# Channel mixing in nine stages that are offset by a quarter of the weights, and some loads and stores on ScalarE's queue

## The chip, the cores and the metric

The kernel runs on one core of a Trainium2 chip. The metric is the device time of one execution in microseconds (us), and the figure quoted is the median over several runs. One execution of the kernel before was also profiled; all rows below come from that one. The engines are called as in the profile: PE (TensorE matmul), PEld (its weight load), DVE (VectorE), ACT (ScalarE), POOL (GpSimd), SP (SyncE, which here only issues DMAs).

## What is computed

Causal attention over 4 batches, 12 heads, 448 positions and 64 columns a head, and behind it a mixer: a two-layer product along the tokens (448 to 256 to 448) and one along the channels (768 to 1536 to 768), each with a relu and a residual.

```python
scores = scale * np.matmul(q, k.transpose(0, 1, 3, 2))
scores = np.where(mask, -1000000000.0, scores)
attn = np.exp(scores - np.max(scores, axis=-1, keepdims=True))
attn = attn / (np.sum(attn, axis=-1, keepdims=True) + 1e-09)
x = np.matmul(attn, v)                                  # heads side by side: (4, 448, 768)
h = np.maximum(x.transpose(0, 2, 1) @ w_tok1, 0.0) @ w_tok2
u = x + h.transpose(0, 2, 1)
h2 = np.maximum(u @ w_ch1, 0.0) @ w_ch2
return (u + h2).astype(np.float32)
```

The four weight matrices arrive as 64-bit floats and are narrowed to 32 bits on the chip.

## The kernel before

The whole kernel is one list of jobs for a planner. `plan.job(costs, fn, needs, holds, rank, moved)` describes a piece of work: which engines may do it and at what assumed cost in ns, what must be done before, which buffers it holds, its rank, and for DMA jobs the assumed time of the transfer. `Plan.emit` (lines 137 to 240) plays the engines forward on those assumed costs: whenever an engine is free it takes the ready job of the lowest rank whose buffers are open. This fixes each engine's instruction order when the kernel is built; nothing is chosen at run time. A buffer ring (`Ring`, `Slot`) hands out its buffers strictly in the order in which the slots were created. While PE has nothing to do in the first 75 us of the plan, a filler matmul is put in (line 536).

Attention goes by 24 pairs of heads (g = 0 to 23, six to a batch) with rank about 2g. A pair has loads of k, q and v on SP's queue (lines 565, 574 and 578; four DMAs for k, four for q, three for v), 32x32 transposes of k and q on DVE (L595), the scores on PE (L623), the row minimum on DVE (L638), the exponential on ACT (L650), a normalisation, the transposes of the probabilities (on PE for the first twelve pairs, L707; by DMA for the last twelve, L761), the product with v (L809), and a transpose of the result on PE (L855). After every second pair of a batch a third of the token mixing follows (L901, L934). When a batch is through, `split_u` writes its u as a high and a low half (uh, ul) for the channel products; the ring for these has two slots, so two batches at a time.

Channel mixing multiplies in three passes (high by high, low by high, high by low), all on line 982, 128x128 by 128x448 each. The hidden 1536 columns go in four quarters. A quarter needs six weight tiles: three of w_ch1 for the upward products (18 matmuls per batch and tile, then relu to gh on ACT, L1015, and the low half gl on DVE, L1018) and three of w_ch2 for the downward ones (two output tiles of 9 matmuls per batch and weight tile, added to u on DVE, L1046). A batch's downward products of a quarter need all three gh and gl of that quarter. Batches go in two groups: 0 and 1, then 2 and 3. Within a group each weight tile serves both batches before the next comes, and the quarters follow each other. In the first group a weight tile is loaded raw (L393), narrowed in one pass on ACT (L396) and two on DVE (L402, L406), saved to a scratch in DRAM (L471), and split into wh (mostly POOL, L339) and wl (DVE or POOL, L348); in the second group it is read back from the scratch (L477) and split again. The rings hold two wf, two wh and two wl, one raw tile, and six gh and gl. Weight tile n of the first group has rank 22 + n (24 tiles); its products run from rank 33 to 57, those of the second group from 57 to 81.

After the last quarter each of the six 128-column tiles of a batch is transposed on DVE (L1093) and stored with four DMAs on SP's queue (L1097). The last tile of batch 3 goes another way, `finish`: two halves, each added (L1065), transposed on PE (L1071), evacuated (L337) and sent with one DMA (L1079).

Of the kernel before, what the change touches and what calls it, by code (L numbers as in the profile page):

```python
# [82 lines left out]
class Plan:  # L83
# [53 lines left out]
    def emit(self):  # L137
# [27 lines left out]
        while left:  # L165
# [3 lines left out]
            for e in self.ENGINES:  # L169
# [42 lines left out]
                free[e] = end  # L212
                if e == "pe":
                    self.spans.append((now, end))
                if e == "sp":
                    dma = end = max(end + 650.0, dma) + pick.moved
                    end += 800.0
                heapq.heappush(events, (end, 0, pick.order, pick))
# [25 lines left out]
def kernel(  # L244
# [11 lines left out]
    nc = tc.nc  # L256
# [12 lines left out]
    NTH = NT // NX  # L269
    NM = DT // P  # L270

    NB = 2
    NQT = 4
    NF = DC // P // NQT
    NW = 2 * NF * NQT
# [17 lines left out]
    def slot(tag):  # L293
        return plan.slot(tag, BUFS[tag])
# [78 lines left out]


    WRANK = -5.0
    CLEAD, WLEAD, TRANK = -9.0, 2.0, 3.5

    def narrow(n, shape, source, f, rank, needs=(), raw=None):

# [66 lines left out]
    scratch = dram.tile([NW, P, NT * P], F32, name="scratch")  # L446
    saved = {}

    def channel_weights(n):

        m = n % NW
        rank = WRANK + 1e-3 * n if n >= NW else NB * H * (1.0 + float(n) / NW) - WLEAD
        qt, o = divmod(m, 2 * NF)
        f, wh, wl = slot("wf"), slot("wh"), slot("wl")
        size = P * NT * P * 4
        if n < NW:
            def source():
                if o < NF:
                    c = qt * NF + o
                    return [w_ch1[:, 2 * c * P:2 * (c + 1) * P].rearrange("(t p) f -> p t f", p=P)]  # L460
                c, t = qt * NF, 2 * (o - NF)
                src = w_ch2[c * P:(c + NF) * P, 2 * t * P:2 * (t + 2) * P]
                return [src.rearrange("(f p) t -> p f t", p=P)]


            shape = [P, NT, P] if o < NF else [P, NF, 2 * P]

            got = [narrow(NT * P, shape, source, f, rank, token_ready)]
            saved[m] = plan.job(
                {"sp": 520.0},  # L470
                lambda e: nc.sync.dma_start(out=scratch[m], in_=flat(f.tile)),  # L471
                got, [f], rank, moved=move(size),
            )
        else:
            got = [plan.job(
                {"sp": 520.0},
                lambda e: nc.sync.dma_start(  # L477
                    out=flat(make(f, [P, NT, P], F32)), in_=scratch[m]
                ),
                [saved[m]], [f], rank, moved=move(size),  # L480
            )]
        a = plan.job(
            {"act": act_sb(NT * P), "pool": pool1(NT * P)},
            lambda e: copy(e, make(wh, [P, NT * P], F32R), flat(f.tile)), got, [f, wh], rank,
        )
        b = plan.job(
            {"pool": pool2(NT * P), "dve": dve1(NT * P)},
            lambda e: minus(e, make(wl, [P, NT * P], F32R), flat(f.tile), wh.tile.bitcast(F32)),
            [a], [f, wh, wl], rank, lock=True,
        )  # L490
        return wh, wl, a, b
# [33 lines left out]
    xs = {}  # L525

    SPARE = 10
    VL = 2.5
    zero = const.tile([P, QC], F32, name="zero")
    nc.vector.memset(zero, 0.0)  # L530
# [25 lines left out]
    def load_pair(g):  # L556
        b, t = divmod(g, NT)
        for nm, src in (("k", k), ("q", q), ("v", v)):
            s = slot({"k": "gh", "q": "gl"}[nm] if 0 < g < SPARE and nm != "v" else "vraw" if nm == "v" else "kq")

            def blocks(e, s=s, src=src):
                make(s, [P, S // 32, 32], F32)
                for n in range(4):
                    j, o = divmod(n, 2)
                    nc.sync.dma_start(  # L565
                        out=s.tile[32 * n:32 * n + 32],
                        in_=src[b, 2 * t + j, :, 32 * o:32 * o + 32].rearrange("(c i) d -> i c d", i=32),
                    )
# [11 lines left out]
                )  # L580

            fn, n = (load, 3) if nm == "v" else (blocks, 4)
            js = [plan.job({"sp": 520.0 * n}, fn, holds=[s], rank=2.0 * g + RL + (VL if nm == "v" else 0.0), moved=1274.0)]
            raws[g, nm] = s, js

    def prep(g):
# [381 lines left out]
                fa, fc = a, c  # L968
            u_split[b, t] = a, c

    def channels(group):

        bs = range(group * NB, (group + 1) * NB)
        total = float(NQT * NB * (NF * NT + NT * NF))
        count = 0
        adds = {}

        def product(ps, w, at, rows, n):

# [8 lines left out]
        def place(n):  # L988
            nonlocal count
            count += n  # L990
            return NB * H * (group + 1 + (count - n) / total) - CLEAD

        for qt in range(NQT):
            gs = {b: [] for b in bs}
            for o in range(NF):
                wh, wl, wa, wb = channel_weights(group * NW + qt * 2 * NF + o)
                for b in bs:
                    uh, ul = us[b]
                    ps = share("m")
                    gh, gl = slot("gh"), slot("gl")  # L1000
                    prev = None
                    for part in range(3):
                        def up(e, part=part, ps=ps, w=(wh, wl, NT), uh=uh, ul=ul):
                            if part == 0:
                                bank(ps)
                            ts = (2 * part, 2 * part + 1)
                            product(ps, w, [t * P for t in ts], [(uh.tile[:, t], ul.tile[:, t]) for t in ts], ts[0])

                        needs = [x for t in (2 * part, 2 * part + 1) for x in u_split[b, t]]
                        prev = plan.job(  # L1010
                            {"pe": pe(*[S] * 6)}, up, needs + [wa, wb, prev], [ps, wh, wl, uh, ul, gh, gl], place(2)
                        )

                    def relu(e, ps=ps, gh=gh):
                        nc.scalar.activation(make(gh, [P, S], F32R), ps.tile[:, :S], AF.Relu)  # L1015

                    def lo(e, ps=ps, gh=gh, gl=gl):
                        nc.vector.scalar_tensor_tensor(  # L1018
                            make(gl, [P, S], F32R), ps.tile[:, :S], 0.0, gh.tile.bitcast(F32),
                            op0=ALU.max, op1=ALU.subtract,  # L1020
                        )

                    a = plan.job({"act": act_ps(S)}, relu, [prev], [ps, gh], WRANK - 1)
                    c = plan.job({"dve": dve1(S)}, lo, [a], [ps, gh, gl], WRANK - 1)
                    gs[b].append((gh, gl, a, c))
            for o in range(NF):
                wh, wl, wa, wb = channel_weights(group * NW + qt * 2 * NF + NF + o)
                for i in range(2):
                    for b in bs:
                        t = 2 * o + i  # L1030
                        ps = share("m")

                        def down(e, ps=ps, w=(wh, wl, NF), i=i, rows=gs[b]):
                            bank(ps)
                            product(
                                ps, w, [(2 * f + i) * P for f in range(NF)], [(x[0].tile, x[1].tile) for x in rows], 0
                            )

                        prev = plan.job(
                            {"pe": pe(*[S] * 9)}, down, [x for r in gs[b] for x in r[2:]] + [wa, wb],  # L1040
                            [ps, wh, wl] + [x for r in gs[b] for x in r[:2]], place(NF),
                        )

                        def plus(e, b=b, t=t, ps=ps):
                            u = utile[b].tile[:, t, :]
                            eng[e].tensor_tensor(u, ps.tile[:, :S], u, op=ALU.add)  # L1046

                        ready = [prev, adds.get((b, t))] + list(u_split[b, t])
                        if (b, qt, t) == (B - 1, NQT - 1, NT - 1):
                            finish(b, t, ps, ready)  # L1050
                            continue
                        adds[b, t] = plan.job({"dve": dve1(S)}, plus, ready, [ps, utile[b]], WRANK - 1)
                        if qt == NQT - 1:
                            store(b, t, adds[b, t])

    def finish(b, t, ps, ready):

        n = NCH // 2
        for part in range(2):
# [16 lines left out]
                copy(e, make(o, [CP, n * P], F32), pt.tile[:CP, :n * P])  # L1076

            def send(e, span=span, o=o):
                nc.sync.dma_start(  # L1079
                    out=out[b, span, t * P:(t + 1) * P].rearrange("(c p) d -> p c d", p=CP),  # L1080
                    in_=o.tile.rearrange("p (c d) -> p c d", c=n),
                )
# [1 line left out]
            a = plan.job({"dve": dve1(n * CP)}, plus, ready, [ps, utile[b]], WRANK - 1)  # L1084
            a = plan.job({"pe": pe(0, 0)}, turn, [a], [pt, utile[b]], WRANK - 1)
            a = plan.job({"act": act_ps(n * P), "dve": dve1(n * P)}, evac, [a], [pt, o], WRANK - 1)
            plan.job({"sp": 520.0}, send, [a], [o], WRANK - 1, moved=n * 320.0)

    def store(b, t, ready):
        o = slot("kq")  # L1090
# [3 lines left out]

        def send(e):
            for n in range(4):
                nc.sync.dma_start(  # L1097
                    out=out[b, :, t * P + 32 * n:t * P + 32 * n + 32].rearrange("(c i) d -> i c d", i=32),
                    in_=o.tile[32 * n:32 * n + 32].rearrange("p (c d) -> p c d", d=32),
                )  # L1100

        a = plan.job({"dve": dve1(S)}, turn, [ready], [utile[b], o], WRANK)
        plan.job({"sp": 2080.0}, send, [a], [o], WRANK, moved=1276.0)

    for g in range(NPAIR):
        load_pair(g)
# [8 lines left out]
            tokens(b, t // NTH)  # L1115
        if t == NT - 1:
            split_u(b)
    for group in range(B // NB):
        channels(group)
    with tc.manual_schedule():  # L1120
        plan.emit()

# [26 lines left out]
```

## Time and profile before

| what | us |
|---|---|
| median of 3 runs (585.39 to 587.37) | 586.76 |
| the profiled execution | 585.49 |
| its span, first to last instruction | 583.7 |
| PE busy in the span | 561.4 (96%) |
| DVE / ACT / POOL busy | 342.1 / 287.8 / 191.5 |

A profile page gives, in its parts: the busy time of each engine; the span in 40 equal slices, one digit each, in tenths of the slice (9 is 90% or more); and groups of instructions with their count, their busy time, the mean ns of one, and the idle time ahead of them. In groups and timelines, "out<-in" names the tile written and the tile read, and "[3.06 <-ACT gh]" after an instruction says that its engine sat idle for 3.06 us before it, and what ended that. Matmuls overlap in PE's pipeline: the duration of one is longer than the distance between two. The chain of waits follows the work that ended last back to the start, so its pieces have the distances and not the overlapped durations. A few per cent of the matmul records can be missing.

### The profile page before, as it was taken

How to read it: one execution, taken by the hardware profiler on the slowest of the kernel's cores; microseconds unless marked ns; L12 is line 12 of the kernel's file. 1: busy time of each engine (PE TensorE's matmuls, PEld its weight loads, DVE VectorE, ACT ScalarE, POOL GpSimd, SP SyncE). 2: the span in 40 equal slices, each digit the busy share in tenths (PEclk: the TensorE clock that was granted, in tenths of full speed). 3: DMA queues.
4: the chain of work that ended last, by engine and by line, in shares of the span. 5: the costliest groups of instructions: out<-in, count | busy, mean ns of one | idle time of the engine just before them, and what ended most of it. 6: DMA issues, size and time to landing. Idle time of an engine off the chain costs nothing.

```text
span 583.7 us, 10169 instructions
## 1 busy us (share of the span) xinstructions
PE 561.4 (96%) x3538; PEld 477.4 (82%) x3544; DVE 342.1 (59%) x840; ACT 287.8 (49%) x734; POOL 191.5 (33%) x301
## 2 busy tenths in 40 slices
PE   8699998998899999999999999999999999999994
PEld 4467876887588888888888888999999999999993
DVE  3586568756677777876777784773242242242162
ACT  3589997677786667767656776500100100100100
POOL 3275566434433124222112222832312312312320
PEclk9999999999899999999999999999999999999998
DMA  5776434647986988896987488366121111111145
GB/s 98 157 155 111 101 65 102 171 82 166 201 184 157 251 185 231 183 240 157 194 213 174 107 175 196 93 121 133 55 64 45 55 56 53 54 55 56 54 85 106
DMA packets 227939, 75.00 MB, mean 128 GB/s; under 512 B 206448, under 2 KB 216624, under 8 KB 227888
## 3 DMA queue, kind: packets, MB, share of 16 engines
q1 hardware_dynamic: 227888, 74.35, 56.5%
q8 instruction: 28, 0.46, 0.3%
q14 instruction: 23, 0.19, 0.1%
HBM read 46.79 MB, written 14.94 MB: 106 GB/s over the span
## 4 chain that ended last, share of the span: by engine, by line
PE 84%; SPq 4%; ACT 3%; DMA 3%; DVE 2%; issue 1%; POOL 1%; DVEq 0%; ACTq 0%; POOLq 0%
PE ps L982 60%; PE ps L809 7%; PE ps L934 4%; PE ps L623 4%; PE ps L901 4%; SPq L565 3%; PE ps L707 2%; DMA pt<-prob 2%; PE ps L855 2%; ACT prob L650 1%; DVE prob L638 1%; SPq L393 1%; PE ps L536 1%; ACT pt L337 1%; POOL prob L339 0%
## 5 line engine op out<-in xcount | busy, mean ns | idle before, releaser
L1015 ACT ACTIVATE gh<-ps 128x448 fp32r<-128x448 f32 x48 | 25.9, 542 | 166.7 <-PE ps L982 166.5
L982 PE MATMUL ps<-uh,wh 128*128 128x448 f32 x288 | 108.0, 375 | 0.0
L982 PE MATMUL ps<-uh,wl 128*128 128x448 f32 x288 | 105.8, 367 | 1.2 <-DVE wl L348 1.2
L982 PE MATMUL ps<-gh,wh 128*128 128x448 f32 x288 | 106.8, 371 | 0.0
L982 PE MATMUL ps<-ul,wh 128*128 128x448 f32 x288 | 105.9, 368 | 0.0
L982 PE MATMUL ps<-gl,wh 128*128 128x448 f32 x288 | 105.4, 366 | 0.0
L982 PE MATMUL ps<-gh,wl 128*128 128x448 f32 x288 | 105.3, 366 | 0.0
L650 ACT ACTIVATE prob<-prob,stat 128x448 f32<-128x448 f32 (+6 forms) x168 | 84.1, 507 | 24.5 <-DVE stat L638 21.9
L1046 DVE TENSOR_TENSOR u<-ps,u 128x448 f32<-128x448 f32 x95 | 59.2, 623 | 61.2 <-PE ps L982 60.3
L339 POOL TENSOR_SCALAR wh<-wf 128x768 fp32r<-128x768 f32 x40 | 33.4, 836 | 166.1 <-PE ps L982 138.7
L339 POOL TENSOR_SCALAR prob<-prob,stat 128x384 f32<-128x384 f32 (+6 forms) x124 | 66.8, 553 | 45.7 <-DVE stat L672 45.2
L1018 DVE SCALAR_TENSOR_TENSOR gl<-ps,gh 128x448 fp32r<-128x448 f32 x48 | 29.7, 620 | 77.9 <-ACT gh L1015 77.9
L638 DVE CUSTOM_DVE_ANT_0 prob<-ps,mask 128x448 f32<-128x448 f32 (+6 forms) x168 | 62.5, 410 | 1.8 <-PE ps L623 1.8
L982 PEld LDWEIGHTS ps<-uh,wl 128*128 128x128 f32 x288 | 54.1, 188 | 6.6 <-DVE wl L348 1.5
L982 PEld LDWEIGHTS ps<-uh,wh 128*128 128x128 f32 x288 | 54.1, 188 | 5.3
L982 PEld LDWEIGHTS ps<-ul,wh 128*128 128x128 f32 x288 | 54.1, 188 | 4.9 <-POOL ul L348 0.3
L982 PEld LDWEIGHTS ps<-gh,wh 128*128 128x128 f32 x288 | 54.0, 188 | 4.9
L982 PEld LDWEIGHTS ps<-gh,wl 128*128 128x128 f32 x288 | 54.1, 188 | 4.8
L982 PEld LDWEIGHTS ps<-gl,wh 128*128 128x128 f32 x288 | 54.1, 188 | 4.4
L809 PE MATMUL ps<-pt,vraw 128*64 128x448 f32 (+3 forms) x384 | 51.6, 399 | 1.3 <-ACT pt L337 1.3
L669 POOL TENSOR_SCALAR stat<-stat 128x3 f32<-128x3 f32 (+1 forms) x45 | 11.1, 248 | 126.3 <-ACT prob L650 125.2
L809 PEld LDWEIGHTS ps<-pt,vraw 128*64 128x64 f32 (+1 forms) x384 | 23.6, 137 | 31.2 <-issue 19.0
(82 smaller groups left out, 908.1 us busy)
## 6 DMA issues: line engine op xcount, KB each, us to landing
wraw<-in_moe_w_ch_dram SPq DMA_DIRECT2D x24, 768.0 KB, 5.2
scratch<-wf SPq DMA_DIRECT2D x24, 384.0 KB, 5.7
wf<-scratch SPq DMA_DIRECT2D x24, 384.0 KB, 3.1
out_dram<-kq SPq DMA_DIRECT2D x92, 56.0 KB, 1.8
vraw<-in_v_dram SPq DMA_DIRECT2D x48, 96.0 KB, 2.5
kq<-in_k_dram SPq DMA_DIRECT2D x60, 56.0 KB, 3.3
kq<-in_q_dram SPq DMA_DIRECT2D x60, 56.0 KB, 2.4
gh<-in_k_dram SPq DMA_DIRECT2D x36, 56.0 KB, 2.5
```

The lines of the kernel that those rows point to most:

```text
L339: eng[e].tensor_scalar(dst, src, scale, 0.0, op0=ALU.mult, op1=ALU.add)
L565: nc.sync.dma_start(out=s.tile[32 * n:32 * n + 32], in_=src[b, 2 * t + j, :, 32 * o:32 * o + 32].rearrange("(c i) d -> i c d", i=32),)
L623: nc.tensor.matmul(scores[r].tile[lanes, WHERE[c]:WHERE[c] + wide(c)], lhsT=qe.tile[LANES[j], c * QC:(c + 1) * QC], rhs=ke.tile[LANES[j], ...
L638: nc.vector.tensor_tensor_reduce(out=part(c, r), in0=ps.tile[:, WHERE[c]:WHERE[c] + wide(c)], in1=mask[:, S - wide(c):], scale=-SCALE, sca ...
L650: nc.scalar.activation(part(c, r), part(c, r), AF.Exp, bias=stat.tile[:, 0, AT[c]:AT[c] + 1], scale=-1.0, accum_out=stat.tile[:, 1, AT[c]: ...
L809: nc.tensor.matmul(ps.tile[LANES[j], c * QC:(c + nq) * QC], lhsT=s.tile[:rows, kb, j], rhs=view[:rows, o:o + nq, j], start=(kb == 0), stop ...
L901: nc.tensor.matmul(ps.tile[:, :PART], lhsT=w[:, c, m * P:(m + 1) * P], rhs=x.tile[:, c, :], start=(n == 0), stop=(n == len(work) - 1),)
L934: nc.tensor.matmul(ps.tile[:, :S], lhsT=h.tile[:, m, o * P:(o + 1) * P], rhs=w[:, m, :], start=(n == 0), stop=(n == 3 * NM - 1),)
L982: nc.tensor.matmul(ps.tile[:, :S], lhsT=x.tile[:, at_:at_ + P], rhs=y, start=(n == 0 and i == 0), stop=(n + 1 == w[2] and i == 2),)
L1015: nc.scalar.activation(make(gh, [P, S], F32R), ps.tile[:, :S], AF.Relu)
L1018: nc.vector.scalar_tensor_tensor(make(gl, [P, S], F32R), ps.tile[:, :S], 0.0, gh.tile.bitcast(F32), op0=ALU.max, op1=ALU.subtract,)
L1046: eng[e].tensor_tensor(u, ps.tile[:, :S], u, op=ALU.add)
```

## The change

The two groups of four quarters become nine stages, each one quarter of the weights for one or two batches. Batch 0 does the first quarter alone; then batches 0 and 1 do the other three; batches 1 and 2 share the first quarter (1's last, 2's first); batches 2 and 3 do the other three; batch 3 does the first quarter alone at the end. The number of matmuls is the same; weight tiles are prepared 54 times instead of 48. The first-time tiles have ranks from 12 on, one rank per tile, and the products of stage s start at rank 27 + 6s. `begun` counts how many quarters a batch's tile has had, so that the fourth one triggers the store. In `finish` the first half's DMA goes to ACT's queue, the second's to SP's. Stores of batches 2 and 3 alternate by tile: even ones on ACT's queue, odd ones on SP's. The q load of pair 0 is issued by ACT. The planner's cost model counts the transfer for any job with a `moved` time, not only for SP's.

```diff
-                if e == "sp":
+                if pick.moved:
                     dma = end = max(end + 650.0, dma) + pick.moved
...
     NB = 2
+    STAGES = ((0, (0,)), (1, (0, 1)), (2, (0, 1)), (3, (0, 1)), (0, (1, 2)), (1, (2, 3)), (2, (2, 3)), (3, (2, 3)), (0, (3,)))
...
-    CLEAD, WLEAD, TRANK = -9.0, 2.0, 3.5
+    CRANK, CSTEP, CLEAD, WLEAD, TRANK = 2.0 * H - 6.0, 6.0, -9.0, 6.0, 3.5
...
-    def channel_weights(n):
-
-        m = n % NW
-        rank = WRANK + 1e-3 * n if n >= NW else NB * H * (1.0 + float(n) / NW) - WLEAD
-        qt, o = divmod(m, 2 * NF)
+    def channel_weights(stage, o):
+
+        qt = STAGES[stage][0]
+        m = qt * 2 * NF + o
+        rank = CRANK + CSTEP * (stage + float(o) / (2 * NF)) - WLEAD if stage < NQT else WRANK + 1e-2 * stage
...
-        if n < NW:
+        if stage < NQT:
...
+    FIRSTQ = 1
...
-                    nc.sync.dma_start(
+                    eng[e].dma_start(
                         out=s.tile[32 * n:32 * n + 32],
...
-            js = [plan.job({"sp": 520.0 * n}, fn, holds=[s], rank=2.0 * g + RL + (VL if nm == "v" else 0.0), moved=1274.0)]
+
+            by = "act" if nm == "q" and g < FIRSTQ else "sp"
+            js = [plan.job({by: 520.0 * n}, fn, holds=[s], rank=2.0 * g + RL + (VL if nm == "v" else 0.0), moved=1274.0)]
...
-    def channels(group):
-
-        bs = range(group * NB, (group + 1) * NB)
-        total = float(NQT * NB * (NF * NT + NT * NF))
+    begun = {}
+
+    def channels(stage):
+
+        qt, bs = STAGES[stage]
+        total = float(len(bs) * (NF * NT + NT * NF))
...
-            return NB * H * (group + 1 + (count - n) / total) - CLEAD
+            return CRANK + CSTEP * (stage + (count - n) / total) - CLEAD
...
+                    times, last = begun.get((b, t), (0, None))
+                    ready = [prev, last] + list(u_split[b, t])
+                    if (stage, t) == (len(STAGES) - 1, NT - 1):
+                        finish(b, t, ps, ready)
+                        continue
+                    last = plan.job({"dve": dve1(S)}, plus, ready, [ps, utile[b]], WRANK - 1)
+                    begun[b, t] = times + 1, last
+                    if times + 1 == NQT:
+                        store(b, t, last)
...
-                nc.sync.dma_start(
+                eng[e].dma_start(
                     out=out[b, span, t * P:(t + 1) * P].rearrange("(c p) d -> p c d", p=CP),
...
-            plan.job({"sp": 520.0}, send, [a], [o], WRANK - 1, moved=n * 320.0)
+            plan.job({("act", "sp")[part]: 520.0}, send, [a], [o], WRANK - 1, moved=n * 320.0)
...
-                nc.sync.dma_start(
+                eng[e].dma_start(
                     out=out[b, :, t * P + 32 * n:t * P + 32 * n + 32].rearrange("(c i) d -> i c d", i=32),
...
-        plan.job({"sp": 2080.0}, send, [a], [o], WRANK, moved=1276.0)
+
+        by = "act" if b >= B - NB and t % 2 == 0 else "sp"
+        plan.job({by: 2080.0}, send, [a], [o], WRANK, moved=1276.0)
...
-    for group in range(B // NB):
-        channels(group)
+    for stage in range(len(STAGES)):
+        channels(stage)
```

The loops inside `channels` are otherwise as before: for each weight tile, all batches of the stage.

## Rows read from the trace of the kernel before

**Rows 1.** The page: engine totals, the DMA slices, one group of instructions.

```profile
PE 561.4 (96%) x3538; PEld 477.4 (82%) x3544; DVE 342.1 (59%) x840; ACT 287.8 (49%) x734; POOL 191.5 (33%) x301
...
DMA  5776434647986988896987488366121111111145
...
L396 ACT ACTIVATE wf<-wraw 128x768 f32<-128x768 f32 x24 | 21.8, 909 | 7.4 <-DMA wraw<-in_moe_w_ch_dram 4.1 <-DVE gl L1018 1.6 <-DVE wl L348 0.8
```

**Rows 2.** Stretches: length, busy PE, PEld, DVE, ACT, POOL, clock, DMA share, GB/s.

```profile
50.00:90.00 40.00, 39.41 (x376) 32.26 (x377) 24.70 (x90) 37.09 (x120) 22.67 (x48) 1.00 0.41 82
90.00:160.00 70.00, 64.50 (x510) 51.14 (x504) 48.89 (x139) 53.58 (x152) 31.53 (x54) 0.98 0.66 149
160.00:381.00 221.00, 221.00 (x1387) 189.18 (x1388) 163.83 (x386) 151.51 (x336) 64.36 (x99) 1.00 0.79 182
```

**Rows 3.** Chain of waits, some pieces: start, length, engine, tile, line, matmuls.

```profile
87.70 0.87 PE ps L707 x8
...
255.46 2.40 PE ps L934 x12
...
291.46 2.50 PE ps L901 x22
...
297.62 1.66 PE ps L623 x14
...
303.17 2.03 PE ps L809 x16
...
380.84 189.94 PE ps L982 x927
```

**Rows 4.** Stretch 90:160, PE of L623, L809, L901, L934, L707, L855, L982.

```profile
90.00:160.00 70.00, 8.96 (x149) 0.98 0.66 149
90.00:160.00 70.00, 13.85 (x96) 0.98 0.66 149
90.00:160.00 70.00, 9.05 (x66) 0.98 0.66 149
90.00:160.00 70.00, 8.97 (x36) 0.98 0.66 149
90.00:160.00 70.00, 8.88 (x64) 0.98 0.66 149
90.00:160.00 70.00, 3.72 (x24) 0.98 0.66 149
90.00:160.00 70.00, 17.60 (x75) 0.98 0.66 149
```

**Rows 5.** Timeline of the end, SP's queue and ACT: start, length, engine, instruction.

```profile
555.61 22.69 SPq L1097 DMA_DIRECT2D out_dram<-kq  x40
...
579.42 2.03 SPq L1097 DMA_DIRECT2D out_dram<-kq  x4
...
575.40 0.83 ACT L337 ACTIVATE kq<-ps 112x256 f32<-112x256 f32 x2 [22.43 <-PE ps L1071]
```

**Rows 6.** Timeline of the start, SP's queue: the q load of pair 0.

```profile
2.71 2.04 SPq L565 DMA_DIRECT2D kq<-in_q_dram  x4
```

**Rows 7.** Timeline, POOL: last low half of batch 0 and of batch 3.

```profile
89.81 1.15 POOL L348 TENSOR_TENSOR ul<-u,uh 128x448 fp32r<-128x448 f32 x1
...
383.42 1.15 POOL L348 TENSOR_TENSOR ul<-u,uh 128x448 fp32r<-128x448 f32 x1
```

**Rows 8.** Timeline, ACT and DVE after the last upward product of batch 3.

```profile
552.43 0.54 ACT L1015 ACTIVATE gh<-ps 128x448 fp32r<-128x448 f32 x1 [3.15 <-PE ps L982]
...
553.01 0.62 DVE L1018 SCALAR_TENSOR_TENSOR gl<-ps,gh 128x448 fp32r<-128x448 f32 x1 [3.06 <-ACT gh L1015]
```

**Rows 9.** Timeline, POOL: the last weight tile is split.

```profile
559.61 0.84 POOL L339 TENSOR_SCALAR wh<-wf 128x768 fp32r<-128x768 f32 x1 [4.56 <-PE ps L982]
560.54 1.84 POOL L348 TENSOR_TENSOR wl<-wf,wh 128x768 fp32r<-128x768 f32 x1
```

**Rows 10.** DMA issues: weight tiles read back, KB each, us to landing.

```profile
wf<-scratch SPq DMA_DIRECT2D x24, 384.0 KB, 3.1
```

More of the change, by code (lines that the diff above doesn't have):

```diff
@@ L969, in split_u @@
             u_split[b, t] = a, c
-    def channels(group):
-        bs = range(group * NB, (group + 1) * NB)
-        total = float(NQT * NB * (NF * NT + NT * NF))
+    begun = {}
+    def channels(stage):
+        qt, bs = STAGES[stage]
+        total = float(len(bs) * (NF * NT + NT * NF))
         count = 0
-        adds = {}
         def product(ps, w, at, rows, n):
@@ L990, in place, with up, relu, lo @@
             count += n
-            return NB * H * (group + 1 + (count - n) / total) - CLEAD
[L993 to L996, printed above, removed]
+            return CRANK + CSTEP * (stage + (count - n) / total) - CLEAD
+        gs = {b: [] for b in bs}
+        for o in range(NF):
+            wh, wl, wa, wb = channel_weights(stage, o)
+            for b in bs:
+                uh, ul = us[b]
+                ps = share("m")
+                gh, gl = slot("gh"), slot("gl")
+                prev = None
+                for part in range(3):
+                    def up(e, part=part, ps=ps, w=(wh, wl, NT), uh=uh, ul=ul):
+                        if part == 0:
+                            bank(ps)
+                        ts = (2 * part, 2 * part + 1)
+                        product(ps, w, [t * P for t in ts], [(uh.tile[:, t], ul.tile[:, t]) for t in ts], ts[0])
+                    needs = [x for t in (2 * part, 2 * part + 1) for x in u_split[b, t]]
+                    prev = plan.job(
+                        {"pe": pe(*[S] * 6)}, up, needs + [wa, wb, prev], [ps, wh, wl, uh, ul, gh, gl], place(2)
+                    )
+                def relu(e, ps=ps, gh=gh):
+                    nc.scalar.activation(make(gh, [P, S], F32R), ps.tile[:, :S], AF.Relu)
+                def lo(e, ps=ps, gh=gh, gl=gl):
+                    nc.vector.scalar_tensor_tensor(
+                        make(gl, [P, S], F32R), ps.tile[:, :S], 0.0, gh.tile.bitcast(F32),
+                        op0=ALU.max, op1=ALU.subtract,
+                    )
+                a = plan.job({"act": act_ps(S)}, relu, [prev], [ps, gh], WRANK - 1)
+                c = plan.job({"dve": dve1(S)}, lo, [a], [ps, gh, gl], WRANK - 1)
+                gs[b].append((gh, gl, a, c))
@@ L997, in channels @@
+        for o in range(NF):
+            wh, wl, wa, wb = channel_weights(stage, NF + o)
+            for i in range(2):
                 for b in bs:
-                    uh, ul = us[b]
+                    t = 2 * o + i
                     ps = share("m")
[L1000 to L1011, printed above, removed]
-                        )
@@ L1014, in relu @@
[L1014 to L1054, printed above, removed]
@@ new lines, in down @@
+                    def down(e, ps=ps, w=(wh, wl, NF), i=i, rows=gs[b]):
+                        bank(ps)
+                        product(
+                            ps, w, [(2 * f + i) * P for f in range(NF)], [(x[0].tile, x[1].tile) for x in rows], 0
+                        )
+                    prev = plan.job(
+                        {"pe": pe(*[S] * 9)}, down, [x for r in gs[b] for x in r[2:]] + [wa, wb],
+                        [ps, wh, wl] + [x for r in gs[b] for x in r[:2]], place(NF),
+                    )
@@ new lines, in plus @@
+                    def plus(e, b=b, t=t, ps=ps):
+                        u = utile[b].tile[:, t, :]
+                        eng[e].tensor_tensor(u, ps.tile[:, :S], u, op=ALU.add)
+                    times, last = begun.get((b, t), (0, None))
[4 more added lines that the diff above has]
+                    last = plan.job({"dve": dve1(S)}, plus, ready, [ps, utile[b]], WRANK - 1)
```

## The prediction

> **What bounds the kernel now.** I read the page's totals first: TensorE (PE) is busy 96% of the span, ScalarE (ACT) about half [rows 1]. An average over such different phases does not say where time can be won, so next came the busy time by stretches. From 160 us on PE has no idle time at all: 221.00 of 221 us up to 381, and behind that the chain of waits is one unbroken run of 927 channel matmuls in 189.94 us, 0.2049 us each [rows 2, 3]. Before that it has holes: 64.50 busy of 70 us between 90 and 160 [rows 2]. So a change wins only in three places: the start, the stretch up to 160, and whatever follows the last matmul.
>
> How much is lost from 90 to 160? Take the instructions of each line in that stretch [rows 4] at the pace that the same lines have in the chain where PE waits for nothing [rows 3]. Scores: 149 records, 28 to a pair (the chain follows 14 of the 28, the others run beside them), 149/28 x 1.66 = 8.8. Attention times v: 96/16 x 2.03 = 12.2. First token product: 66/22 x 2.50 = 7.5. Second: 36/12 x 2.40 = 7.2. Transposes (L707 and L855 together at the pace of L707): 88/8 x 0.87 = 9.6. Channel mixing: 75 x 0.2049 = 15.4. Together 60.7 of 70 us, so 9.3 us of PE's time is lost, 5.5 of it as idle time and the rest in slow restarts.
>
> Behind the last matmul SP is the bound. From 555.61 it issues stores without a pause: 40 in 22.69 us, 0.567 each, so 2.27 us for the four DMAs of one tile, while PE finishes a tile every 9 x 0.2049 = 1.84 us. The final store's four issues end at 579.42 + 2.03 = 581.45, though the last evacuation on ACT is over at 575.40 + 0.83 = 576.23 [rows 5]. The span of 583.7 is 2.25 behind that last issue: its landing.
>
> **The change, part by part** (against the profiled execution, 585.49 us for a span of 583.7; that is 1.27 below the median of 586.76).
>
> *The q load of pair 0 on ACT's queue.* It takes four issues, 2.04 us, off SP [rows 6], which issues without a break in that phase. Everything behind them on SP can start up to 2.04 earlier. On ACT they stand ahead of pair 0's exponentials, which need that load anyway. What could eat it: DMA engines already 50 to 70% busy there [rows 1], and the first attention pairs, which depend on ACT and DVE too. Bounds 0 and -2.1; I take -1.5, near the upper end because SP's queue has no gap there.
>
> *Weights earlier.* The first weight tile of stage 0 has rank 12 where it had 22, five pairs earlier. That puts about three more tiles between 50 and 90 us, each 0.909 us of ACT [rows 1], where ACT is busy 37.09 of 40 [rows 2]. Fully on the path that is +2.7; the planner can move normalisations and evacuations to DVE (24.70 of 40) and POOL (22.67 of 40), then 0. I take +1.5. Batch 0 is ready only at about 90 us, where the last of its low halves is written (89.81 + 1.15) [rows 7], so channel work hides nothing of this.
>
> *Batch 0 alone in stage 0.* Before, the second tile of batch 0 had to follow batch 1 through the rings for gh, gl and the weights; now 3 x 18 + 6 x 9 = 108 matmuls, 22.1 us, wait for batch 0 alone. That is over twice the 9.3 us lost from 90 to 160. Where such filler existed (160 to 381, attention beside it), PE was never idle [rows 2]. So the 5.5 idle us go, and a little of the rest: -6.0. Bounds 0 (the weights or the relu on a busy ACT come too late) and -9.3.
>
> *The middle stages.* Same matmuls at the same pace: 0. Two edges need cover. The uh/ul ring has two slots, so batch 3 can be split only after the last upward product of batch 1 in stage 4. It is needed 18 + 108 + 18 matmuls later, 29.5 us; its six subtractions take 6 x 1.15 = 6.9 on POOL [rows 7]. Batch 2 has the same cover behind stage 3. And batch 3's attention has to be done: in the trace its last low half ends at 384.6 [rows 7]. Stage 4 ends after 108 + 4 x 216 = 972 channel matmuls; 801 (1728 - 927) were done at 380.8 [rows 3], 171 more take 35 us, and with 6 us won stage 5 starts at about 410. 25 us of slack; what comes next if that is gone is PE waiting, microsecond for microsecond.
>
> *Batch 3 alone in stage 8.* Nothing else is left for PE between its last upward product and its first downward one. The chain there is the relu on ACT, then the difference on DVE: from 552.43 to 553.01 + 0.62, 1.2 us [rows 8]; in the kernel before the other batch covers it. A store's four issues ahead of that relu on ACT's queue would add 2.27, but stage 7's last one on ACT is followed by more than a whole upward product, 3.7 us. +1.3, bounds 1.2 and 3.5. Stage 8 also needs six more weight tiles, one per 18 matmuls = 3.69 us instead of 7.38. One tile costs POOL 0.84 + 1.84 [rows 9] and a load that lands 3.1 us after issue [rows 10]; with 0.4 for semaphores 6.2 us in a row. Two buffers give one tile per 3.1 us: hidden, with 0.6 to spare. The price without that cover is a rival below.
>
> *Stores on two queues.* In the last stage only five tiles are stored by fours and one by halves, three of the five on ACT. Each queue gets one tile per two downward products, 2.27 us of issues in 3.69: no backlog. Then the end is the last evacuation (576.23 on the old clock), one issue of 0.5 and a landing of 2.25: 579.0 instead of 583.7. The store of tile 4 sits on ACT just then and may push an evacuation to DVE, 0.3 more. -4.4, bounds -3.0 and -4.8 if the queue is the bound.
>
> Here the Trainium skill speaks against the gain: its page "DMA: Bandwidth & Descriptors", section "Issuing engines are not separate DMA queues", says that transfers started from ScalarE, SyncE and GpSimd share the same 16 engines, and that starting them from several saves only the time of the issue itself, usually small beside the transfer. The trace agrees on what is saved and not that it is small here: 2.27 us of issues for one tile against 2.25 of landing. By the rule's "usually small" this part would be worth nothing and the sum 582.1.
>
> Sum: -1.5 + 1.5 - 6.0 + 1.3 - 4.4 = -9.1 us. The profiled execution would go to 576.4, the median to 577.7, -1.6%.
>
> **The rivals.**
> 1. *The early filling doesn't come.* What speaks for it: ACT is 93% busy from 50 to 90, and each first-time weight tile passes ACT once and DVE twice. If batch 1's attention is pushed back by as much as the channel matmuls fill, the 6.0 are lost: 583.7. Against: PE's queue from 160 on shows that such work fits.
> 2. *The tail is bound by the transfers, not the queue.* Then two queues bring nothing and the end stays 9 us behind the last matmul: 582.1. For: small packets at the end. Against: the DMA engines are 40 to 50% busy in the last two slices [rows 1], and SP's issues follow each other without a gap [rows 5].
> 3. *Slower: stage 8 starves for weights.* If its tiles come one after another, because loads stand behind store issues on SP or a buffer is held too long, each costs 6.2 us against 3.69 of matmuls: 6 x 2.5 = 15 us, 592.7. It decides from 9.1/6 = 1.5 us per tile on, a chain of 5.2 us. Against: two buffers, and no store of stage 8 is due before its downward half.
>
> **How the numbers follow.** Forecast 577.7: 0.62, own range 574 to 581. Rival 1: 0.18, two thirds of it still faster by more than 0.3% (below 585.0), about what a measurement of this kernel can tell from no change. Rival 2: 0.08, faster. Rival 3: 0.08, slower. Others, such as batch 3 coming over 25 us late, 0.04, nearly all slower. Faster: 0.62 + 0.12 + 0.08 = 0.82; same 0.07; slower 0.11. The range takes in the forecast with its bounds (all best ends: -2.1 + 0 - 9.3 + 1.2 - 4.8 = -15, which I don't expect to meet together), rival 2 and most of rival 1: 573 to 585.
>
> **What would show it.** In the profile of the changed kernel: over 100 channel matmuls between 90 and 160 instead of 75, and PE's idle time there under 2 us; PE without a gap up to stage 8, then one of 1.2 to 1.5 us at its middle; the last issue on either queue within 3 us of the last matmul; PE's last channel matmul at about 569 to 570. The prediction is wrong if PE waits for wl or wh in stage 8, if it waits for uh or ul of batch 3 before stage 5, or if the attention of batch 1 ends later by what the channel matmuls gained.

## The result and the profile after

The changed kernel takes 573.37 us (median; 573.04 to 574.31) against 587.07 for the kernel before beside it: ratio 0.9779, 95% interval 0.9759 to 0.98. The profiled execution took 573.29 us with a span of 571.5, so 12.2 us less span than before. The forecast was 577.7 with a range of 573 to 585: right in direction and in the main in its mechanism, 3 to 4 us too small in size. The time lies at the lower edge of that range, and 0.6 us below the 574 to 581 that the prediction gave to its own forecast.

The page after, engine totals, to be read beside [rows 1]:

```profile
PE 557.1 (97%) x3539; PEld 475.4 (83%) x3539; DVE 342.4 (60%) x841; ACT 294.5 (52%) x742; POOL 207.4 (36%) x304
```

PE's busy time hardly says anything: 561.4 became 557.1. The stretches after, to be read beside [rows 2] (length, busy PE, PEld, DVE, ACT, POOL, clock, DMA share, GB/s):

```profile
50.00:90.00 40.00, 39.78 (x358) 32.31 (x356) 27.07 (x95) 36.46 (x111) 24.60 (x43) 1.00 0.57 128
90.00:160.00 70.00, 69.36 (x532) 58.70 (x532) 51.26 (x136) 53.38 (x144) 31.98 (x50) 1.00 0.75 180
160.00:381.00 221.00, 221.00 (x1396) 188.65 (x1396) 159.47 (x386) 153.26 (x350) 75.47 (x106) 1.00 0.83 173
```

Between 90 and 160 us PE is busy 69.36 of 70 us instead of 64.50. By kinds of work, in the order of [rows 4] (here lines 629, 815, 907, 940, 713, 861 and 989):

```profile
90.00:160.00 70.00, 8.87 (x140) 1.00 0.75 180
90.00:160.00 70.00, 10.49 (x80) 1.00 0.75 180
90.00:160.00 70.00, 8.44 (x66) 1.00 0.75 180
90.00:160.00 70.00, 8.03 (x36) 1.00 0.75 180
90.00:160.00 70.00, 8.75 (x65) 1.00 0.75 180
90.00:160.00 70.00, 3.16 (x20) 1.00 0.75 180
90.00:160.00 70.00, 28.65 (x125) 1.00 0.75 180
```

125 channel matmuls stand where 75 stood. At the paces of [rows 3] this is 8.3 + 10.2 + 7.5 + 7.2 + 9.2 + 25.6 = 68.0 us of work in 70: 2.0 us lost instead of 9.3.

A part of these 9.3 us was PE's clock. The granted clock has two levels, 2.4 GHz (1.00 in the rows) and 1.2 GHz (0.50); a stretch can hold some of each. PE's timeline of the kernel before around its longest wait of that stretch, a product with v at the full clock ahead of it, and the stretch of 150 to 155 us (columns as above, the clock third from the end):

```profile
96.52 2.10 PE L809 MATMUL ps<-pt,vraw 128*64 128x448 f32 x16 [0.24 <-ACT pt L337]
...
147.20 0.47 PE L934 MATMUL ps<-w2hi,h1h 128*128 128x448 f32 x1 [2.80 <-ACT h1h L909]
...
148.76 3.37 PE L809 MATMUL ps<-pt,vraw 128*64 128x448 f32 x16
152.05 0.68 PE L934 MATMUL ps<-w2hi,h1h 128*128 128x448 f32 x2
...
150.00:155.00 5.00, 5.00 (x44) 3.36 (x44) 2.02 (x5) 3.35 (x10) 2.03 (x3) 0.86 0.92 263
```

PE stood still for 2.80 us, waiting for h1h, which ACT makes of the first token product. Behind that the granted clock fell (0.79 from 145 to 150, 0.86 from 150 to 155), and a product with v took 3.37 us instead of 2.10. The five matmuls of L934 and this product fill 147.20 to 152.05, 4.85 us; at the paces of [rows 3] they need 3.03. So about 1.8 of the 3.8 us that the prediction called slow restarts were matmuls at the lower clock. In the changed kernel PE stands still for 0.64 us in all between 90 and 160, and the clock stays at 1.00.

The end, timelines of the queues and engines (start, length, engine, instruction), beside [rows 5]: first the last channel matmul of the kernel before, then the changed kernel:

```profile
574.09 0.36 PE L982 MATMUL ps<-gh,wl 128*128 128x448 f32 x1
...
566.11 0.36 PE L989 MATMUL ps<-gh,wl 128*128 128x448 f32 x1
...
567.42 0.76 DVE L341 TENSOR_SCALAR kq<-ps 112x256 f32<-112x256 f32 x2 [0.23 <-PE ps L1079]
...
558.68 9.26 ACTq L1105 DMA_DIRECT2D out_dram<-kq  x12
568.04 0.44 ACTq L1087 DMA_DIRECT2D out_dram<-kq  x1
...
560.52 5.55 SPq L1105 DMA_DIRECT2D out_dram<-kq  x8
568.21 0.32 SPq L1087 DMA_DIRECT2D out_dram<-kq  x1
```

The last channel matmul now ends at 566.47. The evacuation goes to DVE, as foreseen, and both halves of the last tile are issued by 568.53. The span ends 5.0 us behind the last matmul; before it was 9.25 (574.45 to 583.7).

So PE's last matmul comes 8.0 us earlier and the end behind it is 4.2 us shorter.

### The profile page after: what moved, and what is told of

Read it like the earlier page. It is cut to its first block, busy times and chain, and to the rows that moved or that the text cites. A ratio compares the mean times of both kernels' runs of the same rounds, so it can differ in the third digit from the quotient of the medians.

```text
span 571.5 us, 10201 instructions
## 1 busy us (share of the span) xinstructions
PE 557.1 (97%) x3539; PEld 475.4 (83%) x3539; DVE 342.4 (60%) x841; ACT 294.5 (52%) x742; POOL 207.4 (36%) x304
## 4 chain that ended last, share of the span: by engine, by line
PE 89%; DMA 3%; SPq 3%; ACT 2%; DVE 1%; issue 1%; POOL 0%; DVEq 0%; ACTq 0%
PE ps L989 62%; PE ps L815 7%; PE ps L940 5%; PE ps L907 5%; PE ps L629 5%; PE ps L713 2%; PE ps L861 2%; SPq L569 2%; DMA wraw<-in_moe_w_ch_dram 1%; DMA wl<-in_moe_w_tok_dram 1%; ACT prob L656 1%; DMA gh<-in_k_dram 1%; SPq L396 1%; ACT wf L399 0%; DMA kq<-in_q_dram 0%
## 5 line engine op out<-in xcount | busy, mean ns | idle before, releaser
L341 POOL TENSOR_SCALAR wh<-wf 128x768 fp32r<-128x768 f32 x48 | 40.4, 841 | 197.9 <-PE ps L989 161.5
L341 POOL TENSOR_SCALAR prob<-prob,stat 128x448 f32<-128x448 f32 (+6 forms) x125 | 68.4, 561 | 40.0 <-DVE stat L678 34.5
L815 PE MATMUL ps<-pt,vraw 128*64 128x448 f32 (+3 forms) x384 | 50.3, 391 | 1.1 <-ACT pt L339 1.1
L345 ACT COPY pt<-pt 128x512 uint16<-128x512 uint16 (+1 forms) x55 | 42.9, 848 | 14.9 <-DMA pt<-prob 14.8
L815 PEld LDWEIGHTS ps<-pt,vraw 128*64 128x64 f32 (+1 forms) x384 | 23.2, 135 | 30.5 <-issue 18.7
```

What stands on the lines that cost most here:

```text
L341: eng[e].tensor_scalar(dst, src, scale, 0.0, op0=ALU.mult, op1=ALU.add)
L345: nc.scalar.copy(out, in_)
L815: nc.tensor.matmul(ps.tile[LANES[j], c * QC:(c + nq) * QC], lhsT=s.tile[:rows, kb, j], rhs=view[:rows, o:o + nq, j], start=(kb == 0), stop ...
```

## Experiments

Each run that was measured more than once states its ratio to the kernel before, measured beside it on the same chip. "Lost" is PE's time less the work in a stretch at the paces of [rows 3], worked out as above for every run; "up to 50" counts from 7 us on.

**The queues alone, twice.** First all of the queue part in the kernel before:

```diff
+ by = "act" if nm == "q" and g < 1 else "sp"          # load_pair
+ plan.job({("act", "sp")[part]: 520.0}, send, ...)    # finish
+ by = "act" if b >= B - NB and t % 2 == 0 else "sp"   # store
```

> The kernel before, in two groups, with the queue part of the change alone (q load of pair 0, half the stores of batches 2 and 3 and one half of the last tile on ACT's queue). If the end was bound by SP's issues: the distance from the last channel matmul to the end falls from 9.25 us to about 5, and the start gains 0 to 1, so 587.1 goes to 581 to 583. If the transfers themselves were the bound (rival 2): the end stays, 586 to 587.

584.78 us, ratio 0.9975 (0.9948 to 1.0001): no clear gain, and short of the 581 to 583 expected. The end behind the last matmul did shrink, to 5.3 us (578.27 to 583.6), but the last matmul came 3.8 us later than before; PE lost 11 us from 125 to 200 us instead of 7.5. Moving one load at the start had made the planner choose another order everywhere; in it, PE's wait for h1h, 2.80 us before, is 4.91 us long, and the clock behind it is 0.50 from 150 to 155 us instead of 0.86. So the tail alone followed, without the q load, which leaves the order of all engines untouched up to the last quarter:

> The kernel before with half the stores of batches 2 and 3 and one half of the last tile on ACT's queue, and nothing else; the q load of pair 0 stays on SP, so that the order of all engines is that of the kernel before up to the last quarter. Theory: the end is 5 to 5.5 us behind the last channel matmul instead of 9.25, and PE's last matmul stays, so 3.7 to 4.2 us come out: ratio 0.993 to 0.994. That the queues-only run gained just 0.25% was then the new order of work between 125 and 200 us. Rival: ACT's issues hold up something else, and the gain stays under 2 us.

582.58 us, ratio 0.9948 (0.9927 to 0.9969). The end of that run, beside [rows 5]:

```profile
576.21 0.36 PE L982 MATMUL ps<-gh,wl 128*128 128x448 f32 x1
...
559.81 18.32 ACTq L1097 DMA_DIRECT2D out_dram<-kq  x20
...
561.39 16.63 SPq L1097 DMA_DIRECT2D out_dram<-kq  x20
```

Span 581.9, so 5.3 us behind the last matmul: 3.9 less than before, and rival 2 (the transfers bind) falls. The time gained 3.1 us (1.8 to 4.3). The row on PE shows something else: with an unchanged order its last channel matmul ended at 576.57 instead of 574.45. Nearly all of this arose at one place, the wait for h1h and the lower clock behind it, here in this run:

```profile
148.02 0.74 PE L934 MATMUL ps<-w2hi,h1h 128*128 128x448 f32 x1 [3.10 <-ACT h1h L909]
...
150.19 3.88 PE L809 MATMUL ps<-pt,vraw 128*64 128x448 f32 x16
...
150.00:155.00 5.00, 5.00 (x21) 2.50 (x21) 1.33 (x4) 2.79 (x10) 2.26 (x4) 0.56 0.90 218
```

The wait ended 0.8 us later than in the kernel before, the clock from 150 to 155 was 0.56 instead of 0.86, and the next matmul of L934 came at 154.00 instead of 152.05. Differences of up to 2 us between single profiled executions therefore prove nothing by themselves.

**The stages alone**: the changed kernel with every load and store on SP.

```diff
-    FIRSTQ = 1
+    FIRSTQ = 0
-    by = "act" if b >= B - NB and t % 2 == 0 else "sp"
+    by = "sp"
-    {("act", "sp")[part]: 520.0}
+    {"sp": 520.0}
```

> The changed kernel with every load and store on SP's queue: the stages alone. Theory: the 7.4 us lost on PE between 90 and 160 us come back (last channel matmul at 566 to 567.5), and since only five tiles instead of eleven are stored at 1.84 us each at the end, SP's backlog shrinks from 11 x 0.43 = 4.7 us to 5 x 0.43 = 2.2, so the end is 6.5 to 7 us behind the last matmul: 575 to 578. Rival: the stages have nothing to do with the end, which stays at 9.25: 578.5 to 580.

575.74 us, ratio 0.9836 (0.9809 to 0.9862). The last matmul ended at 567.85 and the span 6.25 us later. The offset alone takes 3.0 of the 4.2 us off the end, a little more than expected; the reason given beforehand is that the last stage stores one batch's tiles and not two batches' in turn. The second queue adds the last 1.2. Both parts remove the same backlog, so their gains must not be added: 3.0 + 3.9 is more than there was.

**The q load of pair 0 back on SP** (`FIRSTQ = 0` alone).

> The changed kernel with the q load of pair 0 back on SP's queue. By the accounting of PE's lost time up to 50 us (17.4 before, 16.75 after) it costs 0.6 us: 574.0. By the predicted term it costs 1.5: 574.9. If the first phase were bound by SP's issues alone, 2.0: 575.4.

574.81 us, ratio 0.9817 (0.9796 to 0.9838), span 573.7 in the profiled execution, the slowest of four. PE lost 18.5 us up to 50 and 3.9 from 50 to 90; in the changed kernel 16.8 and 2.8. So the load on ACT is worth 1.4 us by the medians (574.81 against 573.37), 2.2 by the ratios (0.0038 of 587, their intervals just overlap) and 2.8 by lost time. That speaks against the 0.6; between 1.5 and 2.0 the run can't tell. PE's clock is part of it, too: with the load on SP PE stands still for 3.70 us at about 25 to 28.7, and the granted clock is 0.76 from 25 to 30 and 0.55 from 30 to 35; in the changed kernel no wait there is over 0.90 us and the clock is 1.00. And without the load on ACT the start is worse than in the kernel before (17.4 and 2.8), by 2.2 us; the stages-alone run, also with every load on SP, lost 18.0 and 4.0, so 1.8 more, and the run below with early tiles and without the stages 2.0 more. These 1.8 to 2.2 us are the price of the early weight tiles.

**Three q loads on ACT** (`FIRSTQ = 3`).

> The changed kernel with the q loads of pairs 0 to 2 on ACT's queue instead of pair 0 alone; 4.1 us more of issues leave SP. If the first 50 us are bound by SP's issues: 1 to 4 us faster, 569.5 to 572.5. If they are bound by the chain through DVE, ACT and the token weights, as the small gain of the first q load says: within 0.7 us of 573.4; the exponentials queued behind ACT's issues could even make it slower.

576.68 us, ratio 0.9835 (0.9803 to 0.9866): about 3 us slower than the change and slower than both ranges, though that it might be slower was said. ACT's timeline at its start:

```profile
0.71 2.05 ACTq L569 DMA_DIRECT2D gl<-in_q_dram  x4
3.00 2.39 ACTq L569 DMA_DIRECT2D kq<-in_q_dram  x4
5.49 3.24 ACTq L569 DMA_DIRECT2D gl<-in_q_dram  x4
...
10.90 0.67 ACT L656 ACTIVATE prob<-prob,stat 128x448 f32<-128x448 f32 x1 [0.86 <-DVE stat L644]
```

The four issues of a load grow from 2.05 to 3.24 us, and the first exponential comes at 10.90 (10.25 in the changed kernel). SP's issues alone do not bind the start. PE lost 18.7 us up to 50 and 5.7 from 50 to 90 (16.8 and 2.8 in the changed kernel); what in the new order costs this was not followed up.

**The gap in stage 8.** Forecast: 1.2 to 1.5 us between the upward and the downward half. In the changed kernel it isn't there. Timelines of ACT, DVE and PE around that place, beside [rows 8]:

```profile
555.38 0.55 ACT L1021 ACTIVATE gh<-ps 128x448 fp32r<-128x448 f32 x1 [3.15 <-PE ps L989]
...
555.96 0.62 DVE L1024 SCALAR_TENSOR_TENSOR gl<-ps,gh 128x448 fp32r<-128x448 f32 x1 [3.07 <-ACT gh L1021]
...
555.12 0.36 PE L989 MATMUL ps<-gh,wh 128*128 128x448 f32 x1
...
556.33 0.37 PE L989 MATMUL ps<-gh,wh 128*128 128x448 f32 x1
556.63 0.47 PE L989 MATMUL ps<-gl,wh 128*128 128x448 f32 x1
```

PE starts the first downward product at 555.12, before the relu of the last hidden tile has begun at 555.38. The planner's job waits for all three hidden tiles, but each matmul waits only for what it reads: the first six read the two older tiles and last 6 x 0.205 = 1.2 us, just as long as relu and difference take. Only the eighth (it reads the last gl) comes 0.1 us late. To test it, stage 8 took the hidden tiles in reverse:

```diff
+ fs = range(NF)[::-1] if stage == len(STAGES) - 1 else range(NF)
- product(ps, w, [(2 * f + i) * P for f in range(NF)], [(x[0].tile, x[1].tile) for x in rows], 0)
+ product(ps, w, [(2 * f + i) * P for f in fs], [(rows[f][0].tile, rows[f][1].tile) for f in fs], 0)
```

> In stage 8 alone the downward products take the hidden tiles in reverse, the one that is made last first. Theory: the gap forecast between the upward and the downward half (relu and difference, 1.2 us) did not show because the first six matmuls of a downward product need only the two earlier hidden tiles, 6 x 0.205 = 1.23 us; with the order reversed PE stops for 1.1 to 1.4 us there, and the time is 0.8 to 1.3 us longer. Rival: something else hides it (another tile's work): no gap over 0.3 us.

574.79 us in one execution, span 573.0 (571.5 for the change). PE's timeline there:

```profile
555.17 0.37 PE L989 MATMUL ps<-uh,wl 128*128 128x448 f32 x1
556.33 0.44 PE L989 MATMUL ps<-gh,wh 128*128 128x448 f32 x1 [0.79 <-POOL wh L341]
556.89 0.47 PE L989 MATMUL ps<-gl,wh 128*128 128x448 f32 x1
```

From one matmul to the next 1.16 and 0.56 us instead of 0.205 each: 1.3 us of gap, the size that I had forecast. The cause named in the row is the last event the profile could attach; the wh in question had been ready long before. The arithmetic of the term was right, its place on the path was not.

**One buffer for the weight tiles of stage 8.**

```diff
- f, wh, wl = slot("wf"), slot("wh"), slot("wl")
+ f, wh, wl = slot("wf" if stage < len(STAGES) - 1 else "xh"), slot("wh"), slot("wl")
```

> The changed kernel with one buffer instead of two for the weight tiles read back in stage 8. This prices rival 3: a tile's load (3.1), its two halves on POOL or DVE (0.84 and 0.96 to 1.84) and the semaphores (0.4) then come one after another, 5.3 to 6.2 us against 3.69 of matmuls. Four of the six tiles are late by 1.6 to 2.5 us: PE waits 6 to 10 us in stage 8, 580 to 584. If the time stays within 1 us of 573.4, the tiles had far more room than I worked out.

579.55 us in one execution, just under the 580 to 584 expected; the last matmul at 572.85, 6.4 us later than with two. The chain of waits (start, length, what) now runs through the tiles one after another:

```profile
546.50 3.27 DMA xh<-scratch
...
549.95 0.84 POOL wh L341
...
550.81 0.97 DVE wl L350
...
551.80 2.91 DMA xh<-scratch
```

5.3 us from one load to the next, the lower end of what was worked out; the steps between load, halves and next load add up to 0.2 us, not 0.4. With two buffers PE never waits for wh or wl in stage 8: rival 3 has its price right and its condition absent.

**Weight tiles at the old ranks.** The changed kernel with first-time tiles from rank 22 on:

```diff
- CRANK, CSTEP, CLEAD, WLEAD, TRANK = 2.0 * H - 6.0, 6.0, -9.0, 6.0, 3.5
+ CRANK, CSTEP, CLEAD, WLEAD, TRANK = 2.0 * H - 6.0, 6.0, -9.0, -4.0, 3.5
```

> The changed kernel with the first-time weight tiles at rank 22 and on, as in the kernel before, instead of 12 and on; stages as changed. Theory: stage 0 can fill PE's holes from 85 us on only because its tiles are ready by then; with the tiles late, a part of the 7.4 us is lost again: 575 to 579, and under 90 channel matmuls from 90 to 160 us instead of 125. Rival: early tiles are not needed, and ACT is relieved from 50 to 90 us: 571 to 573.4.

591.08 us, ratio 1.0077 (1.0052 to 1.0101): slower than before the change, far outside both expectations. From 90 to 160 PE loses 9.8 us (9.3 in the kernel before), and from 160 to 200 another 10.9 (0.6 before). SP's timeline there, the loads of first-time tiles:

```profile
164.86 0.39 SPq L396 DMA_DIRECT2D wraw<-in_moe_w_ch_dram  x1
176.43 0.39 SPq L396 DMA_DIRECT2D wraw<-in_moe_w_ch_dram  x1
186.76 0.42 SPq L396 DMA_DIRECT2D wraw<-in_moe_w_ch_dram  x1
196.68 0.44 SPq L396 DMA_DIRECT2D wraw<-in_moe_w_ch_dram  x1
```

And the channel matmuls of that stretch (length, busy PE and count, clock, DMA share, GB/s):

```profile
160.00:200.00 40.00, 18.24 (x78) 0.91 0.84 192
```

One tile per 10.6 us. That the single raw buffer sets this pace, through load, ACT and DVE in turn, is argued and was not tried. A tile that serves one batch gives 18 matmuls, so four tiles in 40 us feed 72: 78 were done. With two batches to a tile it is 36; the changed kernel, with one tile per 11 us, has 134 in this stretch:

```profile
160.00:200.00 40.00, 28.90 (x134) 1.00 0.86 185
```

So a stage of one batch spends six scarce tiles on half the work. It pays only when its tiles were loaded before PE needed them.

**The early ranks without the offset**: the kernel before with `WLEAD = 12.0` instead of 2.0.

> The kernel before, in its two groups, with only the ranks of the first-time weight tiles moved from 22 and on to 12 and on. Together with the kernel before, the late-weights run and the changed kernel this makes the square of offset by early tiles. Theory: two wh/wl slots hold the first two tiles until batch 1 has used them, so early tiles cannot serve batch 0 further, and they cost ACT and DVE about 2 us up to 90 us: 586 to 590, no gain. Rival: the early tiles are the gain by themselves and the offset adds little: 577 to 581.

599.25 us, ratio 1.0219 (1.0196 to 1.0242): the slowest of all, again beyond both expectations. Up to 90 us PE loses 22.2 (20.2 before), as expected; from 90 to 160 it loses 7.0 (9.3 before). The rest goes at the change of groups, where PE loses 15 us between 360 and 440. The chain of waits there, and behind it one line of PE's timeline:

```profile
398.87 3.86 DMA wf<-scratch
...
402.89 0.84 POOL wh L339
...
410.35 2.03 PE ps L809 x16
...
421.49 1.14 POOL ul L348
```

```profile
403.77 0.74 PE L982 MATMUL ps<-uh,wh 128*128 128x448 f32 x1 [8.21 <-POOL wh L339]
```

The products of group 0 ran ahead of the attention and were used up. The first tile read back for group 1 had been issued ahead of the stores of batches 0 and 1 on SP; the second was issued behind them, at 398.87, and PE stood still for 8.2 us until it had landed and wh was made. The clock behind that wait was 0.57 from 405 to 410. The last pair's product with v ran only at 410, so batch 3's last low halves were begun from 421 on instead of at 383 [rows 7].

With both runs the square is complete: groups and late tiles 1, groups and early tiles 1.022, offset and late tiles 1.008, offset and early tiles 0.978. Each part alone loses; only together they win. (The offset rows carry the queue part too; its stores alone were worth 0.5% in the kernel before. They also carry earlier ranks of the products, 27 and on instead of 33 and on, so the square doesn't part the offset from those; and the loss of groups with early tiles is mainly one of SP's order at the change of groups, which another placing of the read-backs might avoid. Neither was tried.)

**The offset by half**: batch 0 alone for two quarters, batch 3 for two at the end.

```diff
+ STAGES = ((0, (0,)), (1, (0,)), (2, (0, 1)), (3, (0, 1)), (0, (1, 2)), (1, (1, 2)), (2, (2, 3)), (3, (2, 3)), (0, (3,)), (1, (3,)))
```

> Ten stages instead of nine: batch 0 does two quarters alone, batch 3 the same two at the end (an offset by half). Theory: PE's lost time from 90 to 160 us is already down to 1.6 us, mostly restarts between kinds of work, so twice the filler has nothing left to fill: 573.4 within 1 us. Rival: filler is still short there: 571.5 to 572.5. If the six further weight tiles hurt: above 575.

582.83 us, ratio 0.9944 (0.9926 to 0.9962), 9 us slower than the change. Up to 160 us it is the same, 1.8 us lost from 90 to 160; from 160 to 200 it loses 8.6 us with 101 channel matmuls: twelve tiles are now spent on one batch, and the supply of one per 11 us binds again.

**Tiles three ranks earlier still** (`WLEAD = 9.0` in the changed kernel).

> The changed kernel with the first-time weight tiles at rank 9 and on instead of 12. Theory: stage 0 finds its tiles in time already, so three ranks more only press on ACT and DVE before 90 us: 573 to 576. Rival: stages 0 and 1 are still held by tile supply: 570 to 572.5.

577.92 us, ratio 0.9856 (0.9825 to 0.9886), above both expectations. From 90 to 160 only 1.2 us is lost, but 19.6 up to 50 and 4.7 from 50 to 90: 4.7 more than with rank 12. The rank 12 of the change lies between too late and too early.

**Eight raw buffers for the token weights.**

```diff
- raw=slot(("wh", "wl")[n % 2])
+ raw=slot(("wh", "wl", "uh", "ul")[n % 4])
```

> The changed kernel with the eight raw token-weight tiles in eight buffers instead of four (the rings of uh and ul lend four, unused then). In the changed kernel PE still loses 16.75 us up to 50 us, and the chain there goes twice through the landing of a token weight, 3.1 and 3.3 us. If these landings hold the start: 569 to 572. If the new order spoils as much as the earlier landing gives, as small edits of the order did in other runs: 572 to 576.

576.67 us, ratio 0.9831 (0.9794 to 0.9869), just above both expectations. PE lost 19.0 us up to 50 us. Whether the earlier landings gave something that the new order took away is open. No version was faster than the change.

## Why the prediction was right, point by point

- **The filling** (-6.0): 9.3 us lost became 2.0, so -7.3. The working by paces and counts held; what I left for restarts was too much. About 1.8 of those 3.8 us were matmuls at the lower clock behind PE's wait of 2.80 us, and they went with the wait. The prediction had the clock in its rows (0.98 in [rows 2]) and no term for it.
- **The end** (-4.4): 9.25 became 5.03, -4.2. By step the cause is shared: the offset alone brings 3.0, the queues alone 3.9. I had put the whole under the queues. The sentence on "usually small" issue time in the Trainium skill's page "DMA: Bandwidth & Descriptors", section "Issuing engines are not separate DMA queues", would have made this part nothing; in the tail run the end is 3.9 us shorter with nothing changed but the queue that issues.
- **The q load** (-1.5) and **the early tiles** (+1.5): -1.4 to -2.8 and +1.8 to +2.2, by the run with q on SP against the change and against the kernel before. They nearly cancel, as forecast: up to 90 us PE lost 20.2 before and 19.6 after. At this size a single profile carries an uncertainty of up to 2 us.
- **Batch 3 alone in stage 8** (+1.3): 0.1. This is the step that failed. I read the wait off the job list, where a downward product waits for all three hidden tiles, and not off the instructions, which wait one by one.
- Together -0.6 (the start) - 7.3 + 0.1 - 4.2 = -12.0 against -12.2 measured in the span. This closes because all of it is read from the same two profiles; it is no check of each term. Of the 3 us that the forecast missed, 1.2 are the gap, 1.3 the filling, the rest the start.
- **The signs named beforehand.** 125 channel matmuls from 90 to 160 (over 100 named), 0.64 us idle there (under 2) and the last issue 2.1 us behind the last matmul (within 3) came. The gap in stage 8 did not, and the last channel matmul came at 566.5 and not at 569 to 570. One sign of being wrong came in part: batch 1's last low half ended at 161.87 us on POOL instead of 156.31. That is 5.6 us later, while 62 more channel matmuls (12.7 us) were done by 160. So rival 1 holds for nearly half of what was gained early, but PE had work all the time and the gain stayed.
- **The bound of the filling** was wrong in kind: I gave 0 for weights that come too late. The run with late tiles shows a loss there, 10.9 us from 160 to 200, because single-batch tiles halve the work per tile. And I listed the early tiles as a cost only, when they are the condition of the gain.
- **The slack of batch 3** (25 us) was mostly gone. A piece of the chain after, and a line of POOL's timeline:

```profile
402.22 164.26 PE ps L989 x801
```

```profile
402.44 2.35 POOL L350 TENSOR_TENSOR ul<-u,uh 128x448 fp32r<-128x448 f32 x2 [8.15 <-ACT uh L339]
```

  Batch 3's last low half ends at 404.8, 20 us later than before; I had assumed that it keeps its place. Channel work that runs earlier on a full PE pushes attention back. 1728 - 801 = 927 matmuls were done at 402.2, stage 4 ends 45 matmuls later at 411.4, so 7 us were left. The early-tiles run shows what happens at that place without stage 4 in between.

## What to carry to other kernels

When the bounding engine has holes early and none later, earlier work for it is worth the holes, and the price is found where each work item's inputs come from: count how much work one scarce input (here a weight tile every 10 to 11 us) feeds before splitting a stage. A hole can cost more than its idle time, so look at the clock behind it: 2.80 us of waiting cost PE about 4.6 here. Read waits off instructions rather than off the scheduler's jobs, and add up parts of a change only if they do not empty the same backlog. With an order that a planner makes, test a part by an edit that leaves the rest of the order alone, or the new order is measured instead.

## What the runs showed that was not expected

The same order of instructions put PE's last channel matmul at 574.45 in one profiled execution and at 576.57 in another; a wait for h1h and the lower clock behind it made the difference. Four issues of one load on ACT's queue took 2.05, 2.39 and 3.24 us in a row while SP issued beside it, so an issue's cost is no constant. And the two halves of the change, each slower alone by 0.8 and 2.2%, made 2.2% together.
